# Attention into a gated MLP on one core: first keys and queries two tokens a partition, softmax sums by TensorE, value products with queries on partitions

## The chip, the cores and the metric

One core of a Trainium2 chip runs the whole kernel. The metric is device microseconds of one execution. Three runs of the kernel before took 704.2, 705.42 and 707.07 us, median 705.42. The profile is of one more execution, which took 703.89 us.

## The reference

Attention over 4 batches, 8 heads, 768 tokens, heads of 64, all f32. A query sees the keys less than 16 tokens away, and, beside those, one summary of every block of 32 keys (their maximum by component) whose value is the block's mean. Both share one softmax. The output, as 3072 tokens of 512, goes through a product of two linear maps and a third.

```python
k_sum = k.reshape(B, H, nb, block, D).max(axis=3)
v_sum = v.reshape(B, H, nb, block, D).mean(axis=3)
scores_l = scale * np.matmul(q, k.transpose(0, 1, 3, 2))
mask_l = np.abs(pos[:, None] - pos[None, :]) < window
scores_s = scale * np.einsum('bhsd,bhnd->bhsn', q, k_sum)
scores_s = scores_s + np.log(block)
...
a = a / (np.sum(a, axis=-1, keepdims=True) + 1e-09)
...
a = x @ w_a
b = x @ w_b
return (a * b @ w_out).astype(np.float32)
```

x is 3072 x 512, w_a and w_b are 512 x 1536, w_out is 1536 x 512.

## The kernel before, in words

The tokens are cut into 12 units of 256 (u, three to a batch), a unit into two chunks of 128 (g or t). The hidden width is cut into 12 parts of 128 (f). A pair (u, f) is an item: 24 products of 128x128 by 256 columns (the ups, L959), a multiplication on DVE, a split in a high and a low part on ACT and DVE, and 6 products of 512 columns (the downs, L995). Items of units 0 and 1 alternate while the weights come in; then each unit runs its 12 items. Numbers keep near f32 precision by a split in two fp32r parts: the weights are split on the chip (`convert`, from L271), 18 tiles j of two parts each: a scaled copy on ACT (L294), four steps on DVE (L309 or L315, L320, L327, L333), a rounding to the first part on ACT (L369), and two steps on POOL (L374, L380). `raw` is a weight tile as it comes from memory, `w` its two parts.

Attention of a chunk: the keys lie transposed in `kT`, 160 columns for each 128 tokens, with copies of the summaries in them (L436). For units 0 and 1 (`first_attention`, from L769) nothing is there yet, and the chain is this. Six loads bring 128 tokens of keys each, a token to a partition; TensorE turns each by four transposes (`turn`, L401) into a PSUM bank; ACT copies it into `kT` in two pieces (L460, L462) and DVE takes the blocks' maxima (L470). The queries are turned in the same way and scaled on ACT (L833). TensorE puts the mask into two banks by a product with the identity (L598) and adds the scores (L610, 16 products of 64x64 tiles, four beside each other). DVE takes the maximum of each row (L643), ACT the exponentials with their sums (L655, eight for each chunk, each followed by a read of its accumulator), DVE adds 1e-9 (L664), inverts (L670) and makes diagonal matrices of the result (L677). TensorE turns and scales the weights in one product with these (L698), ACT copies them (L710), TensorE multiplies by the values (L739; the result has channels on partitions, which the items need), and ACT and DVE split it (L747, L750) into `x`. The block means of the values come from twelve products with a matrix of 1/32 (L852).

Banks: o0 to o3 and c0, c1 (with buffer numbers 71 to 74, 77, 78), h0, h1 (75, 76). During this chain o0 and o1 serve chunks 0 and 2, o2 and o3 chunks 1 and 3, c0 and c1 the conversion of weights.

The order is written out ahead of time by the class `Work` (L22): every operation is recorded with an engine, a rank, an estimated duration and the names that it reads and writes, and `emit` lists them, always for the engine that is free first the ready operation of lowest rank. Each engine then runs its list strictly in order, and so do the loads, which all are issued on SP. The ranks around the change are those of L230 and those given to the loads:

```python
CHAIN, FIRST, CONVERT, NEXT, SOON, PREP, LATER = 0, 1, 2, 2.3, 5, 5.5, 6
...
rank = CONVERT + j / 4
...
for i, rank in enumerate((8, 9, 17, 17.5, 19, 20)):
    load_part(i, rank)
```

FIRST is the rank of unit 0's attention, NEXT unit 1's. A turn (product on TensorE) has rank FIRST too, values and scores rank -1.

Of the kernel before, what the change touches and what calls it, by code (L numbers as in the profile page):

```python
# [9 lines left out]
F32 = mybir.dt.float32  # L10
# [74 lines left out]
def attention_moe(  # L85
# [10 lines left out]
    nc = tc.nc  # L96
# [16 lines left out]
    SIGNS = 2  # L113
    AHEAD = (7, 9, 17)
# [75 lines left out]
    qTs = sb([P, NP, P], "qT")  # L190
    nml = [sb([P, 2, 2, NP], f"nml{i}") for i in range(2)]
# [38 lines left out]
    CHAIN, FIRST, CONVERT, NEXT, SOON, PREP, LATER = 0, 1, 2, 2.3, 5, 5.5, 6  # L230
# [40 lines left out]
    def convert(j):  # L271
# [81 lines left out]
        for hs in spans:  # L353
# [13 lines left out]
            act(  # L367
                rank - 0.5, 0.25 + 0.37 * len(hs), f + rk, hi,
                lambda ms=ms, f8=f8: nc.scalar.copy(out=parted(0)[:, ms], in_=f8),  # L369
            )  # L370
# [73 lines left out]
    def first_keys():  # L444
        n = P // BLK
        for i in range(S // P):
            x, key = spot(i // 2)
            x, key = x[:, i % 2 * 512 : (i % 2 + 1) * 512], key[i % 2]
            load(
                i, 262.0, 215, (), [key], x.rearrange("p (h d) -> p h d", d=D),  # L450
                heads(k[0, :, i * P : (i + 1) * P, :]),
            )
            bk = ("c0", "c1", "o2", "o3")[i % 4]
            pe(FIRST, 0.85, [key], [bk], lambda bk=bk, x=x: turn(bank[bk], x))
            c0 = PER * i

            def put(lo, bk=bk, c0=c0):
                tr = bank[bk].rearrange("p (c x) -> p c x", x=P)
                if lo:
                    nc.scalar.copy(out=kT[:, :, c0 + 16 : c0 + WIN], in_=tr[:, :, : WIN - 16])  # L460
                else:
                    nc.scalar.copy(  # L462
                        out=kT[:, :, c0 + P : c0 + PER + 16], in_=tr[:, :, WIN - 16 :]
                    )

            act(FIRST, 0.43, [bk], [f"kTl{i}"], lambda put=put: put(True))
            act(FIRST, 0.33, [bk], [f"kTh{i}"], lambda put=put: put(False))
            dve(
                FIRST, 0.6, [bk], [f"ksi{i}"],
                lambda bk=bk, i=i: nc.vector.tensor_reduce(  # L470
                    out=ks[:, :, i * n : (i + 1) * n],
                    in_=bank[bk].rearrange("p (c n x) -> p c n x", n=n, x=BLK),
                    axis=AX.X, op=ALU.max,
                ),
            )
# [598 lines left out]
```

## Time and profile before

| | |
|---|---|
| median of three runs | 705.42 us |
| the profiled execution | 703.89 us |
| its span, first to last instruction | 702.2 us |
| PE busy | 682.5 us, 97% |
| DVE busy | 439.8 us, 63% |
| ACT busy | 271.2 us, 39% |
| POOL busy | 182.3 us, 26% |
| mean granted clock of TensorE | 0.995 |
| read from memory, written | 47.12 MB, 6.29 MB |

PE is TensorE's products, PEld its weight loads, which overlap them; DVE is VectorE, ACT ScalarE, POOL GpSimd, SP the engine that issues loads. A row of a group or of the timeline names the line, the engine, the operation, and out<-in by the program's names, then the shape; x and a number counts records, and an f32 product makes two records where a transpose makes one. The ends of products are modelled, and the last of a row includes the way through the array, so that a row is some 0.2 us longer than the time to the next one. "Idle" and an arrow name what the engine waited for.

### The profile page before, as it was taken

Reading aid. Unit: us, or ns where it says so; the run is one execution under the profiler, and the core shown is the slowest. Engines: PE = TensorE matmul, PEld = TensorE weight load, DVE = VectorE, ACT = ScalarE, POOL = GpSimd, SP = SyncE. Lnnn points to the kernel's source line nnn. Section 1 sums busy time; section 2 is a strip of 40 time slices with the busy share of each in tenths; the row PEclk is TensorE's granted clock in tenths of the full one; section 3 lists DMA queues with packets and bytes.
Section 4 is the critical chain, followed back from the end, with each engine's and each line's share of the span. In section 5 each row is a group of like instructions: output and inputs, shape, how many; then the busy total and the mean of one; then the engine's idle time right before and its main releaser. Section 6 shows DMA issues by size and latency. Waiting matters only on the chain.

```text
span 702.2 us, 15117 instructions
## 1 busy us (share of the span) xinstructions
PE 682.5 (97%) x6000; PEld 626.5 (89%) x6000; DVE 439.8 (63%) x992; ACT 271.2 (39%) x815; POOL 182.3 (26%) x220
## 2 busy tenths in 40 slices
PE   6889999999999999999999999999999999999997
PEld 3768998898999999999999999999999999999996
DVE  2899899897767777767665776762762662311221
ACT  2998787532424332333332323332331431211211
POOL 5269878652442440113110101110110110000000
PEclk9989999999999999999999999999999999999999
DMA  9989835165224245132210330310310100000000
GB/s 227 280 182 291 301 80 155 27 141 125 64 74 98 70 99 116 32 58 78 54 24 17 69 67 2 87 24 1 84 24 1 54 21 1 31 1 1 31 1 31
DMA packets 154943, 54.84 MB, mean 78 GB/s; under 512 B 132456, under 2 KB 147816, under 8 KB 154872
## 3 DMA queue, kind: packets, MB, share of 16 engines
q1 hardware_dynamic: 154872, 53.88, 32.0%
q8 instruction: 47, 0.77, 0.5%
q14 instruction: 24, 0.20, 0.1%
HBM read 47.12 MB, written 6.29 MB: 76 GB/s over the span
## 4 chain that ended last, share of the span: by engine, by line
PE 85%; DVE 7%; ACT 4%; DMA 2%; issue 1%; POOL 0%; SPq 0%; POOLq 0%; DVEq 0%; ACTq 0%
PE h L959 51%; PE o L995 27%; PE c L739 2%; PE c L610 2%; PE o L739 2%; DVE pt L725 1%; DMA raw<-in_moe_w_b_dram 1%; PE o L610 1%; ACT s L655 1%; DVE c L327 1%; ACT c L294 1%; ACT S L294 1%; DVE ksum L470 1%; PE o L598 1%; DVE gl L984 0%
## 5 line engine op out<-in xcount | busy, mean ns | idle before, releaser
L959 PEld LDWEIGHTS h<-x,w 128*128 128x128 f32 x3456 | 413.9, 188 | 10.8 <-DVE c L327 0.2
L959 PE MATMUL h<-x,w 128*128 128x256 f32 x3456 | 416.3, 277 | 0.0
L979 DVE TENSOR_TENSOR h<-h,g 128x256 f32<-128x256 f32 x144 | 62.0, 430 | 163.7 <-ACT g L976 162.4
L976 ACT COPY g<-h 128x256 f32<-128x256 f32 x144 | 53.7, 373 | 277.6 <-PE h L959 276.8
L995 PE MATMUL o<-w,gh 128*128 128x512 f32 x576 | 158.0, 396 | 1.9 <-ACT gh L981 1.9
L995 PEld LDWEIGHTS o<-w,gh 128*128 128x128 f32 x576 | 98.8, 188 | 19.5 <-ACT gh L981 2.7
L725 DVE STREAM_TRANSPOSE pt<-s 32x256 f32<-32x256 f32 x240 | 104.7, 436 | 8.3 <-POOL s L685 4.0
L685 POOL TENSOR_TENSOR s<-s,nml 128x512 f32<-128x512 f32 x40 | 41.7, 1042 | 243.1 <-DVE nml L670 241.5
L995 PE MATMUL o<-w,gl 128*128 128x512 f32 x288 | 89.7, 393 | 0.0
L655 ACT ACTIVATE s<-s,nml 128x128 f32<-128x128 f32 x160 | 62.5, 393 | 49.5 <-DVE nml L643 46.8
L984 DVE TENSOR_TENSOR gl<-h,gh 128x256 fp32r<-128x256 f32 x144 | 60.5, 420 | 29.7 <-ACT gh L981 28.2
L981 ACT CAST gh<-h 128x256 fp32r<-128x256 f32 x144 | 53.5, 372 | 62.9 <-DVE h L979 62.6
L995 PEld LDWEIGHTS o<-w,gl 128*128 128x128 f32 x288 | 53.9, 188 | 11.7
L540 POOL TENSOR_TENSOR S<-S 96x512 f32<-96x512 f32 (+3 forms) x48 | 33.5, 698 | 49.6 <-DMA S<-in_v_dram 39.8
L655 ACT ACTIVATION_READ_ACCUMULATOR s<-s,nml 128x1 f32 x160 | 30.3, 190 | 0.0
L664 DVE TENSOR_SCALAR nml<-nml 128x4 f32<-128x4 f32 x40 | 11.5, 287 | 30.0 <-ACT s L655 30.0
L374 POOL TENSOR_TENSOR space<-space,w 128x1024 f32<-128x1024 f32 (+1 forms) x13 | 26.8, 2058 | 11.8 <-ACT w L369 10.9
L380 POOL TENSOR_TENSOR w<-space 128x1024 fp32r<-128x1024 f32 (+1 forms) x13 | 26.8, 2064 | 1.0
L294 ACT ACTIVATE S<-raw 128x1024 f16<-128x1024 f32 (+1 forms) x20 | 23.1, 1153 | 6.5 <-DVE S L309 4.6
L643 DVE TENSOR_REDUCE nml<-s 128x4 f32<-128x512 f32 x40 | 25.2, 667 | 0.0
L294 ACT ACTIVATE c<-raw 128x512 f32<-128x512 f32 x36 | 23.2, 645 | 4.0 <-DVE space L320 1.5
L436 POOL COPY kT<-ksum 128x144 f32<-128x144 f32 x16 | 4.7, 307 | 61.0 <-DVE ksum L518 55.0
(104 smaller groups left out, 478.0 us busy)
## 6 DMA issues: line engine op xcount, KB each, us to landing
raw<-in_moe_w_a_dram SPq DMA_DIRECT2D x12, 512.0 KB
raw<-in_moe_w_b_dram SPq DMA_DIRECT2D x12, 512.0 KB
raw<-in_moe_w_out_dram SPq DMA_DIRECT2D x12, 512.0 KB
out_dram<-S SPq DMA_DIRECT2D x24, 256.0 KB
qin<-in_q_dram SPq DMA_DIRECT2D x160, 32.0 KB
S<-in_v_dram SPq DMA_DIRECT2D x24, 192.0 KB
vw<-in_v_dram SPq DMA_DIRECT2D x18, 192.0 KB
kin<-in_k_dram SPq DMA_DIRECT2D x24, 100.0 KB
```

The lines of the kernel that those rows point to most:

```text
L294: nc.scalar.mul(out=zhalf[:, lo:hi] if out is None else out, in_=high.bitcast(F32), mul=2.0**-112)
L540: lambda: nc.gpsimd.tensor_tensor(out=out, in0=i0, in1=i1, op=ALU.add),
L655: lambda h=h, c=c, sums=sums: nc.scalar.activation(s[h][:, c, :], x[h][:, c, :], AF.Exp, bias=m[:, 0, h, c : c + 1], scale=1.0, accum_out= ...
L685: lambda h=h, r=r: nc.gpsimd.tensor_tensor(out=s[h], in0=s[h], in1=r[:, :, None].broadcast_to([P, NP, P]), op=ALU.mult,),
L725: lambda js=js, qs=qs: nc.vector.transpose(out=pv[js, :, qs], in_=sv[qs, :, js]),
L739: nc.tensor.matmul(ps[h * D : (h + 1) * D, c, es], vw[e][:, 2 * c + h, :], d[:, h, c, es], start=True, stop=True, tile_position=(0, h * D),)
L959: nc.tensor.matmul(ps, w[:, c, part, :], x[xpart][:, c, :], start=(i == 0), stop=(i == n - 1))
L976: act(CHAIN, 0.38, [hk], [gk], lambda: nc.scalar.copy(out=g, in_=pa))
L979: lambda: nc.vector.tensor_tensor(out=pa, in0=pb, in1=g, op=ALU.mult),
L981: act(CHAIN, 0.41, [hk], [ghk], lambda: nc.scalar.copy(out=gh, in_=pa))
L984: lambda: nc.vector.tensor_tensor(out=gl, in0=pa, in1=gh.bitcast(F32), op=ALU.subtract),
L995: nc.tensor.matmul(bank[ok[j]], (gh if first else gl)[:, js], w[:, :, part, :], start=(f == 0 and first and part == 0), stop=(f == NF - 1 ...
```

## The change

- Keys of batch 0 come in three loads of 256 tokens, and the queries of unit 0 in one, with two consecutive tokens a partition, so that a row in memory is 512 bytes, not 256. TensorE turns the even and the odd tokens apart (a half each), by eight products of 64 columns, two beside each other in the array (`turn_paired`, now L465). ACT puts each half into `kT` at every second column by three copies, DVE takes each half's block maxima, and one more operation joins them.
- In the first two units, ACT's exponentials no longer sum. The weights are turned unscaled by transposes; TensorE sums them by products with a column of ones, 1e-9 added by a first product (`total`), and multiplies them with the values so that queries, not channels, lie on partitions (`weigh`). DVE inverts the sums and scales the result, and TensorE turns it back for the split.
- POOL adds the two tokens of a partition of the values first, so the block means need six products, not twelve.
- POOL and not ACT rounds the first parts of weight tiles 0 and 1.
- The masks wait until the first keys are turned; unit 1's rank goes from 2.3 to 1.5, and the first weight tile's loads from ranks 8 and 9 to 5 and 5.5 (the queries have 6). Later units are as before; their code is only written more shortly.

```diff
+    FIRSTS = 2
...
+    ones = sb([P, 1], "ones")
+    nc.vector.memset(ones, 1.0)
+    small = sb([P, H], "small")
+    nc.vector.memset(small, 1e-9)
...
-    CHAIN, FIRST, CONVERT, NEXT, SOON, PREP, LATER = 0, 1, 2, 2.3, 5, 5.5, 6
+    CHAIN, FIRST, CONVERT, NEXT, SOON, PREP, LATER = 0, 1, 2, 1.5, 5, 5.5, 6
...
+            if j < FIRSTS:
+                pool(
+                    rank - 0.5, 0.1 + 0.55 * len(hs), f + rk, hi,
+                    lambda ms=ms, f8=f8: nc.gpsimd.tensor_copy(out=parted(0)[:, ms], in_=f8),
+                )
...
-            bk = ("c0", "c1", "o2", "o3")[i % 4]
-            pe(FIRST, 0.85, [key], [bk], lambda bk=bk, x=x: turn(bank[bk], x))
...
+    def load_paired(rank, key, x, src, row):
+        load(
+            rank, 524.0, 300, (), key, x.rearrange("p (h x) -> p h x", x=2 * D),
+            src[0, :, row : row + 2 * P, :].rearrange("h (p t) d -> p h (t d)", t=2),
+        )
+    def turn_paired(dst, x, y):
+        for c in range(NP):
+            for h in range(2):
+                nc.tensor.matmul(
+                    dst[h * D : (h + 1) * D, c * P : (c + 1) * P], paired(x)[:, 2 * c + h, y, :],
+                    ident, start=True, stop=True, tile_position=(0, h * D),
+                )
+    def first_keys(ksy, mk):
+        n = 2 * P // BLK
+        for m in range(S // P // 2):
+            x, key = spot(m)
+            load_paired(m, key, x, k, 2 * P * m)
+            for y in range(2):
+                bk = ("c0", "c1", "o2", "o3")[(2 * m + y) % 4]
+                pe(
+                    FIRST, 0.85, key, [bk] + ["first"] * (m == 0),
+                    lambda bk=bk, x=x, y=y: turn_paired(bank[bk], x, y),
+                )
...
+                def put(m=m, y=y, bk=bk):
+                    tr = bank[bk].rearrange("p (c i x) -> p c i x", c=NP, x=P // 2)
                     nc.scalar.copy(
+                        out=kper[:, :, 2 * m : 2 * m + 2, 16 + y : WIN : 2], in_=tr[:, :, :, :40]
                     )
+                    for i in range(2):
+                        c0 = PER * (2 * m + i) + P + y
+                        nc.scalar.copy(out=kT[:, :, c0 : c0 + 48 : 2], in_=tr[:, :, i, 40:])
+                act(FIRST, 0.9, [bk], [f"kT{m}{y}"], put)
+                dve(
+                    FIRST, 0.6, [bk, f"kT{m}{y}"], [f"ks{m}{y}"],
+                    lambda bk=bk, m=m, y=y: nc.vector.tensor_reduce(
+                        out=ksy[:, y, :, m * n : (m + 1) * n],
+                        in_=bank[bk].rearrange("p (c n x) -> p c n x", n=n, x=BLK // 2),
+                        axis=AX.X, op=ALU.max,
+                    ),
+                )
...
+        every = [f"{m}{y}" for m in range(3) for y in range(2)]
+        dve(
+            FIRST, 0.2, [f"ks{x}" for x in every] + [mk], [f"ks{c}" for c in range(NP)],
+            lambda: nc.vector.tensor_tensor(
+                out=ks, in0=ksy[:, 0], in1=ksy[:, 1], op=ALU.max
+            ),
+        )
         for c in range(NP):
...
-                d, dk = diag
-                dve(
-                    rank, 0.6, lk + [xk[h]], dk[h],
-                    lambda h=h, r=r, d=d: nc.vector.tensor_tensor(
-                        out=d[:, h], in0=ident[:, None, :].broadcast_to([P, NP, P]),
-                        in1=r[:, :, None].broadcast_to([P, NP, P]), op=ALU.mult,
-                    ),
-                )
...
-            def turned(h):
-                for c in range(NP):
-                    nc.tensor.matmul(
-                        bank[banks[h]][:, c * P : (c + 1) * P], s[h][:, c, :], d[:, h, c, :],
-                        start=True, stop=True,
-                    )
...
+        for h in range(2):
+            pe(
+                rank + 0.1, 0.9, ["first"], [banks[h]],
+                lambda h=h: nc.tensor.matmul(
+                    x[h], ident, mask[:, kind, None, :].broadcast_to([P, NP, P]),
+                    start=True, stop=False,
+                ),
+            )
+        pe(-1, 1.2, [*qk] + KT, banks, lambda: dots(t, qT, banks, False))
...
+                act(
+                    rank, 0.2, [f"{mk}m{h}", banks[h]], [sk[h]],
+                    lambda h=h, c=c: nc.scalar.activation(
+                        s[h][:, c, :], x[h][:, c, :], AF.Exp, bias=m[:, 0, h, c : c + 1]
+                    ),
+                )
...
+        def turned(h):
+            for c in range(NP):
+                nc.tensor.transpose(bank[banks[h]][:, c * P : (c + 1) * P], s[h][:, c, :], ident)
+        for h in range(2):
+            pe(-1, 0.6, [sk[h]], [banks[h]], lambda h=h: turned(h))
+            act(
+                rank, 0.6, [banks[h]], dk[h],
+                lambda h=h: nc.scalar.copy(
+                    out=d[:, h], in_=bank[banks[h]].rearrange("p (c x) -> p c x", x=P)
+                ),
+            )
+        ps = bank[banks[0]].rearrange("p (g d) -> p g d", d=D)
+        sums = bank[banks[1]][:, :H]
+        l = m[:, 1].rearrange("p h c -> p (h c)")
+        xn = s[0].rearrange("p c x -> p (c x)")
+        def total():
+            nc.tensor.matmul(sums, ident, small, start=True, stop=False)
+            for c in range(NP):
+                for h in range(2):
+                    g = 2 * c + h
+                    nc.tensor.matmul(
+                        sums[:, g : g + 1], d[:, h, c, :], ones, start=False, stop=g == H - 1
+                    )
+        def weigh():
+            for c in range(NP):
+                for h in range(2):
+                    g = 2 * c + h
+                    for e in range(2):
+                        es = slice(e * QT, (e + 1) * QT)
+                        nc.tensor.matmul(
+                            ps[es, g, :], d[:, h, c, es], vw[e][:, g, :],
+                            start=True, stop=True, tile_position=(0, e * QT),
+                        )
+        pe(-1, 0.5, dk[0] + dk[1], [banks[1]], total)
+        pe(-1, 1.1, dk[0] + dk[1] + vk, [banks[0]], weigh)
+        dve(
+            rank, 0.15, [banks[1]], [f"{mk}l"],
+            lambda: nc.vector.reciprocal(out=l, in_=sums),
+        )
+        dve(
+            rank, 0.6, [banks[0], f"{mk}l"], [sk[0]],
+            lambda: nc.vector.tensor_tensor(
+                out=xn.rearrange("p (g d) -> p g d", d=D), in0=ps,
+                in1=l[:, :, None].broadcast_to([P, H, D]), op=ALU.mult,
+            ),
+        )
+        pe(-1, 0.6, [sk[0]], [banks[1]], lambda: turn(bank[banks[1]], xn))
+        split(u, t, banks[1])
...
+        ksy = x[:, 512 + P + 16 : 512 + P + 16 + 2 * NP * NS]
+        first_keys(ksy.rearrange("p (t c n) -> p t c n", t=2, c=NP), mk)
+        q0, qk = spot(3)
+        load_paired(6, qk, q0, q, 0)
...
+        for y in range(2):
+            pe(FIRST, 0.85, qk, [f"h{y}"], lambda y=y: turn_paired(bank[f"h{y}"], q0, y))
+            act(
+                FIRST, 0.6, [f"h{y}"], [yk[y]],
+                lambda y=y: nc.scalar.mul(
+                    out=both[:, :, y :: 2],
+                    in_=bank[f"h{y}"].rearrange("p (c x) -> p c x", x=P), mul=0.125,
+                ),
+            )
...
-            for y in range(2):
-                nc.tensor.matmul(
-                    bank["h0"][:, g * 256 : (g + 1) * 256], mean[:, 16 - 8 * i : 16 - 8 * i + P],
-                    vin[n][0][:, :, y * D : (y + 1) * D],
-                    start=(i == y == 0), stop=(i == 2 and y == 1),
-                )
+            nc.tensor.matmul(
+                bank["h0"][:, g * 256 : (g + 1) * 256], mean[:, 16 - 8 * i : 16 - 8 * i + P],
+                vin[n][0][:, :, :D], start=(i == 0), stop=(i == 2),
+            )
 
         for n in range(6):
-            pe(FIRST + 0.5, 1.0, [vin[n][1], mk], ["h0"], lambda n=n: means(n))
+            x, key = vin[n]
+            pool(
+                FIRST, 0.7, [], [key],
+                lambda x=x: nc.gpsimd.tensor_tensor(
+                    out=x[:, :, :D], in0=x[:, :, :D], in1=x[:, :, D:], op=ALU.add
+                ),
+            )
+            pe(FIRST + 0.5, 0.5, [key, mk], ["h0"], lambda n=n: means(n))
...
-    for i, rank in enumerate((8, 9, 17, 17.5, 19, 20)):
+    for i, rank in enumerate((5, 5.5, 17, 17.5, 19, 20)):
```

More of the change, by code (lines that the diff above doesn't have):

```diff
@@ L442, in attention_moe, with paired @@
     KT = [f"kT{c}{x}" for c in range(NP) for x in "ks"]
[L444 to L451, printed above, removed]
-            )
-            bk = ("c0", "c1", "o2", "o3")[i % 4]
-            pe(FIRST, 0.85, [key], [bk], lambda bk=bk, x=x: turn(bank[bk], x))
[L455 to L461, printed above, removed]
+    def paired(x):
+        return x.rearrange("p (h t d) -> p h t d", t=2, d=D)
```

286 lines of the change are left out of this document (122 added, 164 removed).

## The prediction

> **What bounds the kernel now.** I read the stage table first, then TensorE's timeline, then the waits, then the groups by line. The stage table of before (from to: length, busy us of each engine with counts, granted clock, DMA share, GB/s):
>
> ```profile
> 0.00:18.30 18.30, 10.62 (x42) 6.21 (x42) 5.12 (x8) 5.92 (x15) 9.90 (x58) 1.00 1.10 229
> 18.30:62.50 44.20, 38.67 (x420) 31.89 (x421) 41.61 (x79) 40.45 (x110) 25.33 (x17) 0.92 1.00 246
> 62.50:150.00 87.50, 85.63 (x692) 79.19 (x691) 80.74 (x155) 61.26 (x129) 70.92 (x43) 1.00 0.54 151
> 150.00:702.20 552.20, 547.54 (x4851) 509.18 (x4849) 312.37 (x751) 163.52 (x564) 76.11 (x105) 1.00 0.21 48
> ```
>
> The columns are PE, PEld, DVE, ACT, POOL. After 62.5 us PE is busy 99% of the time; from 18.3 to 62.5 DVE is (41.61 of 44.2, 94%), ACT close behind it. TensorE's timeline and its waits from 62 us on give the point where that changes:
>
> ```profile
> 62.54 5.62 PE L959 MATMUL h<-x,w 128*128 128x256 f32 x48
> PE o L995 <- ACT gh L981: 1.9, 2, 1.2
> ```
>
> 62.54 us is the start of item (0,2), the third product item. From there PE runs almost through: it waits 1.9 us at two down-products and little else. The change touches nothing that PE does behind this point, and in both programs PE has issued the same two items ahead of it. So the change is worth what it moves the start of (0,2), plus any new wait behind it. Everything below works out that one time.
>
> One more thing lies in that stretch. The stage table around PE's longest pause there:
>
> ```profile
> 43.60:47.00 3.40, 1.18 (x11) 1.02 (x10) 3.17 (x9) 3.27 (x15) 0.14 (x1) 1.00 0.82 272
> 47.00:53.90 6.90, 6.18 (x52) 5.57 (x51) 6.59 (x12) 6.87 (x15) 5.36 (x3) 0.51 1.18 281
> ```
>
> PE was busy for only 1.18 of 3.4 us, and then had half its clock for 6.9 us.
>
> **The first stage: loads, keys, queries.** Rates (last column) of the first 5 us, and by what SP's issues then brought: 256-byte rows at 2 to 8 us, weights at 12 to 14, 512-byte rows of values at 16 to 18:
>
> ```profile
> 0.00:5.00 5.00, 0.55 (x1) 0.50 (x2) 0.97 (x2) 1.28 (x1) 3.80 (x27) 1.00 0.68 134
> 2.00:8.00 6.00, 3.55 (x4) 1.40 (x5) 0.01 (x1) 0.09 (x1) 4.79 (x29) 1.00 1.24 219
> 12.00:14.00 2.00, 1.08 (x5) 0.71 (x6) 0.90 (x2) 1.01 (x4) 0.00 (x0) 1.00 1.09 339
> 16.00:18.00 2.00, 0.89 (x9) 0.65 (x6) 0.69 (x1) 1.24 (x4) 0.64 (x3) 1.00 1.22 290
> ```
>
> 134 GB/s over 5 us is 0.67 MB, at 219 GB/s 3.1 us: bytes flow from 1.9 us. Two tokens a partition make 512-byte rows. The first of three key loads (0.52 MB at 290) has landed at about 4.0, the last at 7.4. Two weight loads (ranks 5 and 5.5) now pass the queries on SP: 1.05 MB at 339 is 3.1 us, then 1.8 for the queries, 12.4 us. Before: 2.1 MB at 219 from 1.9, 11.5 us. The queries lose 0.9 us, covered by the key turns and masks ahead of them on PE (to 16.4, below); without that cover it would cost the 0.9.
>
> TensorE's prices, from the timeline (start, length, group):
>
> ```profile
> 4.45 3.78 PE L598 MATMUL o<-mask,ident 128*128 128x512 f32 x4 [4.45 <-POOL mask L173]
> 10.68 0.66 PE L401 MATMUL c<-ident,space 128*128 128x128 f32 x4
> 18.29 1.10 PE L610 MATMUL o<-kT,qT 64*64 64x128 f32 x32 [1.40 <-POOL kT L436]
> 19.25 1.10 PE L610 MATMUL o<-kT,space 64*64 64x128 f32 x32
> 23.94 1.13 PE L698 MATMUL o<-pt,s 128*128 128x128 f32 x8
> 28.30 1.03 PE L852 MATMUL h<-space,space 128*128 128x256 f32 x4
> 30.80 1.01 PEld L739 LDWEIGHTS h<-pt,vw 128*64 128x64 f32 x32
> 30.80 1.15 PE L739 MATMUL h<-pt,vw 128*64 128x64 f32 x32
> 34.34 1.98 PE L598 MATMUL o<-mask,ident 128*128 128x512 f32 x4 [0.71 <-ACT qT L833]
> ```
>
> Two masks took 3.78 us at the start and 1.98 later: PE starts at half speed. A turn of 128 tokens (four transposes) is about 0.55 us. The change turns with eight plain products of 64 columns by 128 instead, two records each. One 128-column record is about 0.12 us (L698, eight in 1.13 with the tail). L739 shows 32 records on two column halves in 1.15, 0.03 each for 64 columns, so two run beside each other: 16 records of 0.06 make 0.95 us a half. One after another they would take 1.9; below 0.95 nothing in the trace points.
>
> PE now begins with the first keys at 4.0, not with masks. I let it warm at 9.5, as far behind its first work as the rows allow (the masks were slow from 4.45 to 8.2): 2.9 halves at 1.9 us, then 3.1 at 0.95, end 12.4. ACT's three copies a half and DVE's maximum keep that pace; before, they took turns on one bank:
>
> ```profile
> 10.31 0.32 ACT L462 COPY kT<-c 128x192 f32<-128x192 f32 x1 [0.76 <-DVE ksum L470]
> 10.52 0.43 ACT L460 COPY kT<-c 128x320 f32<-128x320 f32 x1
> 17.36 1.05 POOL L436 COPY kT<-ksum 128x144 f32<-128x144 f32 x4 [5.92 <-DVE ksum L470]
> ```
>
> 0.43 and twice 0.2 is 0.85 us on ACT. The keys' part ends some 3 us earlier, but PE isn't ready to use it: the four masks stand behind the key turns now (4 x 1.0), then two query halves (1.9) and two mean products (1.0): the scores start at 19.3 us, against 18.29. So the early keys gain nothing; the one thing gained is that DVE converts weights meanwhile:
>
> ```order
> L470 TENSOR_REDUCE ksum<-c_78 128x4x4
> L315 TENSOR_SCALAR space_195<-c_77 128x512
> L320 SCALAR_TENSOR_TENSOR space_195<-c_77,space_195 128x512
> L643 TENSOR_REDUCE nml_184<-o_71 128x4
> L643 TENSOR_REDUCE nml_184<-o_72 128x4
> ```
>
> These are DVE's rows up to the first score maxima (L643), before. Now, with L728 the maxima and raw_211 the first weight tile:
>
> ```order
> L499 TENSOR_REDUCE space_196<-c_78 128x4x8
> L508 TENSOR_TENSOR ksum<-space_196 128x96
> L320 TENSOR_SCALAR space_199<-c_77 128x512
> L325 SCALAR_TENSOR_TENSOR space_199<-c_77,space_199 128x512
> L332 TENSOR_SCALAR c_78<-space_199 128x512
> L320 TENSOR_SCALAR space_199<-c_77 128x512
> L338 SCALAR_TENSOR_TENSOR space_199<-raw_211,c_78 128x512
> L325 SCALAR_TENSOR_TENSOR space_199<-c_77,space_199 128x512
> L332 TENSOR_SCALAR c_78<-space_199 128x512
> L338 SCALAR_TENSOR_TENSOR space_199<-raw_211,c_78 128x512
> L728 TENSOR_REDUCE nml_188<-o_71 128x4
> L728 TENSOR_REDUCE nml_188<-o_72 128x4
> ```
>
> Eight conversion steps stand ahead of the maxima, not two.
>
> **The second stage: sums by PE, queries on partitions.** What leaves DVE and ACT, and what POOL pays for such work: groups by line and shape up to 62.5 us (busy, mean ns of one, idle before), and four timeline rows:
>
> ```profile
> L677 DVE TENSOR_TENSOR pt<-ident,o 128x512 f32<-128x512 f32 x4 | 2.7, 687 | 0.2
> L677 DVE TENSOR_TENSOR space<-ident,o 128x512 f32<-128x512 f32 x4 | 2.7, 686 | 0.1
> L670 DVE RECIPROCAL o<-o 128x4 f32<-128x4 f32 x8 | 1.5, 190 | 0.2
> L664 DVE TENSOR_SCALAR o<-o 128x4 f32<-128x4 f32 x8 | 1.3, 165 | 0.2
> L327 DVE TENSOR_SCALAR c<-space 128x512 int32<-128x512 int32 x10 | 6.9, 689 | 0.1
> 20.04 2.47 DVE L643 TENSOR_REDUCE nml<-o 128x4 f32<-128x512 f32 x4
> 20.76 0.37 ACT L655 ACTIVATE s<-o,nml 128x128 f32<-128x128 f32 x1
> 21.02 0.17 ACT L655 ACTIVATION_READ_ACCUMULATOR s<-o,nml 128x1 f32 x1
> 21.22 0.37 ACT L655 ACTIVATE s<-o,nml 128x128 f32<-128x128 f32 x1
> L369 ACT CAST w<-space 128x512 fp32r<-128x512 f32 x4 | 2.4, 613 | 0.0
> L710 ACT COPY pt<-o 128x512 f32<-128x512 f32 x4 | 2.5, 621 | 0.0
> L870 POOL COPY space<-vw 32x512 f32<-32x512 f32 x2 | 1.2, 609 | 11.7 <-ACT vw L864 11.7
> L374 POOL TENSOR_TENSOR space<-space,w 128x512 f32<-128x512 f32 x4 | 5.1, 1284 | 1.9 <-ACT w L369 1.9
> ```
>
> DVE loses 2.7 + 2.7 + 1.5 + 1.3 = 8.2 us and gets four reciprocals (0.19) and four 128x512 products (0.69), 3.5. With the eight early steps (8 x 0.69 = 5.5) its 41.6 us of the stretch become about 31.4. ACT: an exponential and its accumulator take 0.46 us from start to start; alone 0.15 to 0.26 (the accumulator starts 0.26 behind it), I take 0.2, the nearer to the 192-element copy's 0.21. 32 x 0.26 = 8.3 less, and 2.4 of roundings go to POOL: 40.4 becomes under 30. POOL gets four copies (0.61) and six sums of half of L374's size (0.64), 6.3 us on 25.3 of 44.2: hidden, since its first weight parts are due only at item (0,0).
>
> PE gets the difference. For chunk 0, from the means (L852, now L930) to the value products (L739, now L778), before and now; o_71 to o_74 are its PSUM banks:
>
> ```order
> L698 MATMUL o_71<-pt,s 128x128 x4
> L698 MATMUL o_72<-pt,s 128x128 x4
> L852 MATMUL h_75<-space_191,space_192 128x256 x2
> L698 MATMUL o_73<-space_188,space_191 128x128 x4
> L852 MATMUL h_75<-space_191,space_192 128x256 x2
> L401 MATMUL o_71<-ident,space_188 128x128 x4
> L698 MATMUL o_74<-space_188,space_191 128x128 x4
> L739 MATMUL h_76<-pt,vw_165 64x64 x2
> ```
>
> ```order
> L748 MATMUL o_71<-ident,s 128x128 x4
> L748 MATMUL o_72<-ident,s 128x128 x4
> L930 MATMUL h_75<-space_195,space_196 128x256
> L764 MATMUL o_72<-small,ident 128x8
> L768 MATMUL o_72<-ones,pt 128x1 x8
> L778 MATMUL o_71<-vw_165,pt 64x64
> ```
>
> The plain products with a diagonal become transposes (1.0 us a bank to 0.55). New are the sums (L764, L768: nine products, 18 weight loads for hardly a column) and, behind the value products, a turn back of 0.55 (L412). The sums' price: a load and record of 128 columns is at most 0.12 (L698, there bound by the columns), at least twice the 0.03 of a 64-column load (L739): 1.1 to 2.2 us a chunk. I take the middle, 1.65. The Trainium skill (TensorE: Matmul & The Clock Gate, LDWEIGHTS) gives a load its columns divided by 1.2, 107 ns for 128: by that the sums would be 1.9, an estimate from that page. No run here shows such loads without columns behind them.
>
> Ups and downs are from the chain of waits, undisturbed:
>
> ```profile
> 72.50 1.37 PE o L995 x6
> 73.88 2.75 PE h L959 x24
> ```
>
> PE's list from the first scores to (0,2): scores 4 x 0.95, means 4 x 0.5 (half as many products, six fewer, 3 us), turns 8 x 0.55, sums 4 x 1.65, values 4 x 1.05, turns back and of the later queries 6 x 0.55, masks 4 x 1.0, ups 2 x 2.75, downs 2 x 1.37: 3.8 + 2.0 + 4.4 + 6.6 + 4.2 + 3.3 + 4.0 + 5.5 + 2.7 = 36.5 us. That is more than DVE's 31 or ACT's 30: the bound passes to PE, and 19.3 + 36.5 = 55.8 is the floor.
>
> Above the floor stand PE's waits, since the order is fixed. Chunk 0: its scores end at 20.3, two maxima (2.47 / 4 each) and the last exponentials at 22.9, when PE has done chunk 1's scores and three means (22.7): 0.2. Its sums need two copies of ACT with a conversion copy between them, 0.5 each from start to start: 0.9. Its turn back waits 1.0 for DVE, which reads the sums (L787) and then does three conversion steps of 0.69 ahead of the product. Chunk 2's turns: 0.3, for an item's copy among its exponentials. The last stands here, DVE between chunks 2 and 3, before and now:
>
> ```order
> L677 TENSOR_TENSOR pt<-ident,o_71 128x512
> L643 TENSOR_REDUCE nml_185<-o_73 128x4
> L643 TENSOR_REDUCE nml_185<-o_74 128x4
> L979 TENSOR_TENSOR h_75<-h_75,g_173 128x256
> L327 TENSOR_SCALAR c_78<-space_193 128x512
> ```
>
> ```order
> L728 TENSOR_REDUCE nml_189<-o_73 128x4
> L787 RECIPROCAL nml_188<-o_72 128x8
> L728 TENSOR_REDUCE nml_189<-o_74 128x4
> L338 SCALAR_TENSOR_TENSOR S_190<-raw_310,c_78 128x512
> L314 SCALAR_TENSOR_TENSOR space_199<-c_77,S_191 128x512
> ```
>
> Chunk 3's second maximum now queues behind chunk 2's reciprocal, which waits for PE's sums. Behind the sums' end come that reciprocal (0.25), the maximum (0.65), two conversion steps (1.4) that free the bank for a copy of ACT (0.5), and three exponentials behind it (0.75): 3.55 us, in which PE has only the value products (1.05): a wait of 2.5. Sum 4.9 us; (0,2) starts at 60.7, 1.8 earlier than 62.54. The profiled execution took 703.89 us, so 702.1; the median of the three runs shown is 705.42, 1.5 above it, so 703.6.
>
> **Rivals.** *The waits close* (chance 0.34). Sums at 1.1 us take 2.2 off PE's list, and 0.55 each off the waits of chunk 0 and chunk 3; a clock that warms 1.7 us sooner gives 0.9. (0,2) at 56.5, 6.0 off: 699.4. For it speaks that DVE and ACT then have 10 us to spare; against it the fixed order.
>
> *PE's clock falls again* (0.23). The wait of 2.5 us ahead of chunk 3's turns is as long as the pause in the table above (2.2 idle of 3.4) that half clock followed. Then turns, an up and sums run twice as long over 6.9 us: 3.4 us more than forecast, 707.0; with the sums at 2.2 another 3.3, 710.3, slower. The Trainium skill (TensorE: Matmul & The Clock Gate, What's actually happening) has the clock halve after an idle window of about 3.4 us and come back after a busy one; the trace agrees on two such lengths at half clock (6.9 us), but fell with PE busy a third of its window.
>
> *The paired turns don't pair* (0.10), the case on the other side. If the two column halves run one after another, a half is 1.9 us warm. The six key halves end at 18.1 instead of 12.4, the query halves cost 1.9 more: +7.6, so 711.2. It decides from 1.2 us a warm half on (0.95 + 1.8/8); above 1.6 the kernel is measurably slower. L739's 0.03 speaks against it; L468 being no transposes, for it.
>
> **How the numbers follow.** Forecast 0.33, the others 0.34, 0.23, 0.10. About 0.5%, 3.5 us, is what a measurement of this kernel can tell from no change. Faster: 0.34. Same: 0.33 and 0.16 of the clock's. Slower: 0.07 of it and 0.10, 0.17. The range 698.5 to 709 leaves out about 0.1 on either side: the fastest end of the first rival, and the unpaired turns; both signs are in it, and the forecast's own range, with the sums' two ends, is 700 to 707.
>
> **What would show it.** Right: L468 at 0.95 a half when warm, first scores near 19.3, L768 near 1.65 a chunk, L787 waiting for it, PE's pause ahead of chunk 3's L748, (0,2) near 60.7, DVE no longer the busiest from 18 to 62. Wrong: scores before 17 or after 21, no pause there, or new waits of PE behind 62 us on weights (DVE or ACT late).

## The result, and the profile after

The changed kernel took 726.25 us (median of 4 runs, 723.34 to 729.63), the kernel before 705.94 on the same chip (4 runs, 704.20 to 707.07). The ratio is 1.029, interval 1.024 to 1.034: slower by 20 us, far outside the forecast of 698.5 to 709. The profiled execution took 726.35 us, its span is 724.6.

First where the time went. The start of item (0,2) in the timeline after, and the stage table from there to the end, after and then before:

```profile
67.01 5.92 PE L1034 MATMUL h<-x,w 128*128 128x256 f32 x48
```

```profile
67.01:724.60 657.59, 653.07 (x5541) 605.83 (x5539) 390.55 (x904) 225.33 (x693) 146.62 (x147) 1.00 0.24 60
```

```profile
62.54:702.20 639.66, 633.13 (x5541) 588.36 (x5539) 393.11 (x905) 224.75 (x692) 147.00 (x147) 1.00 0.26 62
```

(0,2) starts at 67.01 instead of 62.54, 4.5 us later. Behind it PE handles exactly as many records of products as before (5541), at a granted clock of 1.00 in both, waits less (4.5 us against 6.5), and yet needs 17.9 us more. So four fifths of the loss lie where the prediction had said that nothing could change. The chain of waits shows that it is no stall. The 24 ups of an item, then six downs and the next 24 ups, after (the rows of before have 2.75 and 1.37):

```profile
78.88 2.88 PE h L1034 x24
81.76 1.40 PE o L1070 x6
83.15 2.88 PE h L1034 x24
```

0.13 us more an item, times the 142 items behind (0,2), is 18.5 us: every up is a little slower, all the time. The downs add a little, and the shorter waits take as much off again.

Now the stretch ahead of (0,2), by the stage table of after, with the four windows around the clock's two falls:

```profile
18.30:62.50 44.20, 40.25 (x427) 34.66 (x422) 31.36 (x53) 32.42 (x70) 25.49 (x23) 0.85 0.83 226
...
24.55:27.96 3.41, 2.20 (x19) 1.80 (x17) 1.38 (x2) 3.36 (x7) 2.63 (x4) 1.00 0.94 288
27.96:34.79 6.83, 6.83 (x57) 6.70 (x57) 5.32 (x9) 3.59 (x10) 2.53 (x4) 0.50 0.77 215
...
48.45:51.86 3.41, 3.41 (x68) 3.22 (x58) 2.16 (x6) 2.77 (x4) 2.55 (x2) 1.00 1.14 314
51.86:58.68 6.82, 4.65 (x29) 4.47 (x26) 6.52 (x12) 6.71 (x15) 5.23 (x3) 0.50 0.94 269
```

Before, the clock was halved once in this stretch (6.9 us from 47.0), now twice, 6.83 us each. Ahead of the second fall PE was busy for all of the window (3.41 of 3.41), so a wait in that window can't be its cause. The same two windows for the sums' line alone (length, PE and PEld with counts, granted clock, DMA share, GB/s):

```profile
24.55:27.96 3.41, 1.41 (x13) 1.44 (x13) 1.00 0.94 288
48.45:51.86 3.41, 1.93 (x16) 1.87 (x16) 1.00 1.14 314
```

Most of what PE did ahead of both falls were products with one moving column. The steps of the prediction, in the timeline of after:

```profile
11.39 1.93 PE L468 MATMUL c<-ident,space 128*64 128x128 f32 x32
19.84 0.43 PE L686 MATMUL o<-kT,space 64*64 64x128 f32 x5
...
21.70 2.25 ACT L736 ACTIVATE s<-o,nml 128x128 f32<-128x128 f32 x8 [2.16 <-DVE nml L728]
...
49.08 1.93 PE L768 MATMUL o<-ones,pt 128*128 128x1 f32 x16
...
54.34 1.97 PE L748 MATMUL o<-ident,space 128*128 128x128 f32 x8 [2.17 <-ACT space L736]
```

Two key halves take 1.93 us warm with the tail, 0.97 each, the scores start at 19.84, and the wait ahead of chunk 3's turns is 2.17: these were foreseen at 0.95, 19.3 and 2.5.

### The profile page after: what moved, and what is told of

Its sections match the earlier page's. It is cut to its first block, busy times and chain, and to the rows that moved or that the text cites. A ratio compares the mean times of both kernels' runs of the same rounds, so it can differ in the third digit from the quotient of the medians.

```text
span 724.6 us, 15385 instructions
## 1 busy us (share of the span) xinstructions
PE 711.1 (98%) x6140; PEld 655.3 (90%) x6140; DVE 434.2 (60%) x979; ACT 266.4 (37%) x785; POOL 188.7 (26%) x230
## 4 chain that ended last, share of the span: by engine, by line
PE 90%; DVE 4%; ACT 2%; DMA 2%; issue 1%; SPq 0%; DVEq 0%; ACTq 0%
PE h L1034 52%; PE o L1070 26%; PE c L819 2%; PE o L686 2%; PE c L686 2%; PE o L819 1%; PE o L768 1%; PE o L719 1%; PE c L468 1%; DVE c L332 1%; DVE pt L704 1%; DMA raw<-in_moe_w_b_dram 1%; PE o L748 1%; DMA raw<-in_moe_w_out_dram 1%; ACT s L736 1%
## 5 line engine op out<-in xcount | busy, mean ns | idle before, releaser
L1034 PEld LDWEIGHTS h<-x,w 128*128 128x128 f32 x3456 | 430.8, 189 | 10.9 <-issue 0.3
L1034 PE MATMUL h<-x,w 128*128 128x256 f32 x3456 | 434.4, 283 | 0.0
L1070 PE MATMUL o<-w,gh 128*128 128x512 f32 x576 | 159.7, 399 | 0.7 <-ACT gh L1056 0.6
L666 DVE TENSOR_SCALAR nml<-nml 128x4 f32<-128x4 f32 x40 | 9.4, 234 | 30.0 <-ACT s L658 30.0
```

Source lines behind the costliest of these rows:

```text
L1034: nc.tensor.matmul(ps, w[:, c, part, :], x[xpart][:, c, :], start=(i == 0), stop=(i == n - 1))
L1070: nc.tensor.matmul(bank[ok[j]], (gh if first else gl)[:, js], w[:, :, part, :], start=(f == 0 and first and part == 0), stop=(f == NF - 1 ...
```

## Experiments on the ups: where the weights lie

Theory A: the two new tiles, `ones` (4 bytes a partition) and `small` (32 bytes), lie between `x` and the weight tiles, and in units of 32 bytes they push all weights 64 bytes away from `x`; the ups read both at once. Theory B: something in the changed instruction list slows them. In bytes of a partition, `x` and the first buffer of the weights begin at 31360 and 63936 before and at 31360 and 64000 after, so they lie 32576 and 32640 apart. So the kernel before got an unused tile and nothing else, and the changed kernel one more:

```diff
+    sb([P, 16], "pad")      # before_pad64, after_pad64; [P, 32] in before_pad128
```

In before_padx64 the same 64 bytes stand ahead of `x`, so that `x` and the weights move together.

> The kernel before, unchanged but for the same unused tile of 64 bytes ahead of nml: the weight tiles move to 0 modulo 128, where the changed kernel has them. Theory A: ups at 119 to 120 ns, 144 items x 24 x 5.2 ns = 18 us more, 721 to 726 us. Theory B: 705 us, ups at 114 ns.

> The kernel before with an unused tile of 128 bytes: all behind it moves, but the weights stay at 64 modulo 128. Theory A: no change, 704 to 707 us, ups at 114 ns. If any shift of the weights by itself, or the place modulo 256, slows the ups (theory A2): 721 to 726 us.

> The changed kernel with one unused tile of 64 bytes a partition behind the new tiles ones and small, so that the weight tiles begin at 64 modulo 128 again, as before the change, while x stays at 0. Theory A (the place of the weight tiles against x slows every up, 114 to 119.5 ns): ups back at 114 ns, the 17.9 us behind item (0,2) gone, 0.3 to 0.8% over the kernel before: 707 to 711 us. Theory B (something in the order or the other engines' work of the changed program slows the ups): ups stay at 119 to 120 ns, 724 to 729 us.

> The kernel before with the unused 64 bytes ahead of x: x, g, gh, gl and the weights all move, the weights to 0 modulo 128 and x to 64, so that they stand to each other as before. If the place of the weights against x decides (A, relative): 704 to 707 us, ups at 114 ns. If the place of the weights alone decides (A, absolute): 721 to 726 us, ups at 119 to 120 ns.

Measured against 705.66 us for the kernel before (13 runs): before_pad64 722.05, ratio 1.024 (1.021 to 1.027); before_pad128 718.78, 1.020 (1.015 to 1.024); after_pad64 724.63, 1.027 (1.023 to 1.031); before_padx64 704.71, 0.999 (0.997 to 1.000). The ups of one item by the chain of waits, of before_pad64, before_pad128 and before_padx64:

```profile
317.09 2.88 PE h L960 x24
```

```profile
302.57 2.82 PE h L960 x24
```

```profile
312.46 2.75 PE h L960 x24
```

An unused tile of 64 bytes makes the old kernel as slow in the ups as the changed one, and moving both operands together costs nothing. So the distance counts, and not the list. Two expectations failed: I had taken the effect to repeat with 128 bytes, and it doesn't. By itself after_pad64 lies in the range of Theory B (724 to 729 us); but its weights lie 128 bytes farther from `x` than before, and its ups take 117.8 ns from start to start, as those of before_pad128 do. Then the tiles of the changed kernel were put ahead of `x`:

```diff
+    ones = sb([P, 1], "ones")
+    nc.vector.memset(ones, 1.0)
+    small = sb([P, H], "small")
+    nc.vector.memset(small, 1e-9)
     xs = [[sb([P, NP, CH], f"x{i}_{p}", F32R) for p in range(2)] for i in range(2)]
```

> The changed kernel, its two new tiles (the column of ones and the 1e-9 tile) allocated ahead of x instead of behind it, so that weights and x lie as far apart as in the kernel before (32,576 bytes of a partition). Nothing else is changed. Theory A (the distance of weights and x sets the rate of the ups): ups 114.3 ns from start to start, item period 4.120 us, and behind the start of (0,2) 638 to 640 us, as before; (0,2) itself still starts near 67.0, since the clock still falls twice ahead of it: 706 to 710 us, ratio 1.001 to 1.006. Rival B (something in the changed list behind (0,2) slows the ups): ups near 119.5 ns, 722 to 728 us.

It took 711.42 us (711.07 to 712.22), ratio 1.009 (1.007 to 1.011). The ups and the stage behind the start of (0,2), which in this run is at 68.66:

```profile
300.05 2.75 PE h L1034 x24
```

```profile
68.66:709.40 640.74, 634.16 (x5541) 588.95 (x5539) 393.15 (x904) 225.13 (x693) 146.48 (x147) 1.00 0.25 61
```

640.7 us instead of 657.6, and 2.75 again. Theory B is out: 14.8 us of the 20 came from the place of two tiles of 36 bytes. The total lies just above the range expected (706 to 710 us), and the profiled execution has three falls of the clock ahead of (0,2), not the two expected. Three more distances were tried, on a later version of the kernel (after_mv_wide, below), with an unused tile of 192, 256 and 32 bytes ahead of `nml`, behind `x`:

> As after_mv_wide, with an unused tile of 192 bytes a partition ahead of nml, so that weights and x lie 192 bytes farther apart than in the kernel before. What the distance does is known at 0 (114.3 ns from up to up), 64 (119.5) and 128 (117.8) more. If the rate repeats with 256 bytes and falls off on both sides of a best place, 192 gives about what 64 gave, 118 to 120 ns and 721 to 726 us; if it keeps coming down towards 256 or 512, 114 to 117 ns and 704 to 715 us; if the place before isn't the best one, under 113.5 ns and under 702 us.

> As after_mv_wide, with 256 bytes a partition more between weights and x. If the rate repeats with 256 bytes: 114.3 ns from up to up, 703 to 707 us. If it repeats with 512 bytes (all tiles of weights and x begin a multiple of 512 bytes apart), another rate than at 0: 117 to 121 ns and 714 to 728 us, or, if the place before isn't the best one, under 113.5 ns and under 702 us.

> As after_mv_wide, with 32 bytes a partition more between weights and x. The rate so far: 114.3 ns at 0 and 256 bytes more, 119.5 at 64, 117.8 at 128, 119.7 at 192. If lines of 64 bytes or less count, 32 lies between 0 and 64: 115 to 119 ns, 707 to 722 us. If the place before is not the best, under 113.5 ns and under 702 us. If only whole steps of 64 count, 114.3 ns and 703 to 707 us.

One run each: 723.23, 705.38 and 719.76 us. The first two are what a period of 256 bytes gives, and the third shows that 32 bytes already count. Their ups of an item, in the same order:

```profile
303.56 2.87 PE h L1034 x24
```

```profile
312.99 2.75 PE h L1034 x24
```

```profile
302.94 2.82 PE h L1034 x24
```

All together (mean time from the start of one up, or of one down, to the next within an item, worked out from the records behind 300 us):

```
bytes more than before    0      32     64     128    192    256
ns from up to up          114.3  118.1  119.5  117.8  119.7  114.3
ns from down to down      232.1  236.3  235.5  236.7  235.1  232.2
```

The rate of the ups is the same at 0 and at 256 and 3 to 5% worse at the four distances between. The downs lose 1 to 2% at the same four, where the weights have moved by the same bytes against their other operand (`gh` and `gl`, allocated behind `x`). All pieces of weights and `x` that an up reads begin a multiple of 512 bytes from the start of their tile, and the tiles a multiple of 4096 bytes from the first of their kind, so that one distance holds, but for multiples of 512, for all 3456 ups. The Trainium skill (TensorE: Matmul & The Clock Gate, Step-by-step: what each phase is for) has two independent read ports, so that loading the next weights takes nothing from the product that runs. These runs disagree: with nothing but the distance changed, an up costs up to 5.4 ns more. Which of the two reads is held up, and what in the memory makes 256 bytes special, wasn't tried.

## Experiments on the clock

Theory C: a window of 3.41 us filled mostly with one-column products counts as idle. Rival D: PE's waits alone make the clock fall. All kernels here start from after_mv. after_mv_wide widens the sums' products (the loads and their number stay):

```diff
-    ones = sb([P, 1], "ones")
+    ones = sb([P, D], "ones")
...
-            nc.tensor.matmul(sums, ident, small, start=True, stop=False)
...
-                        sums[:, g : g + 1], d[:, h, c, :], ones, start=False, stop=g == H - 1
+                        wide[:, 2 * c + h, :], d[:, h, c, :], ones, start=True, stop=True
```

> As after_mv, but each product of the sums moves 64 columns of ones instead of one (the 1e-9 that a first product adds is left out; the sums stand in every 64th column). As many weight loads and as many products. Theory C (a window full of one-column products counts as idle for the clock): neither of the two falls of the clock at 28 and 52 us, or at most one, (0,2) starts at 60.5 to 63.8, the sums take about as long in the warm clock, 699 to 705 us. Rival D (the clock falls because PE waits for ACT and DVE in these stretches, whatever the products' width): two falls as in after_mv, (0,2) at 67 or later, 706 to 712 us.

It took 704.61 us (10 runs, 702.40 to 706.18), 6.8 less than after_mv; against the kernel before 0.998 (0.996 to 1.000). Its profile, which is of the fastest of the ten executions, has no fall:

```profile
18.30:60.64 42.34, 37.77 (x455) 31.37 (x453) 33.60 (x58) 32.87 (x70) 29.19 (x23) 1.00 1.01 246
...
24.95 2.00 PE L767 MATMUL o<-ones,pt 128*128 128x64 f32 x16 [1.21 <-ACT pt L754]
60.64 5.62 PE L1033 MATMUL h<-x,w 128*128 128x256 f32 x48
```

64 columns take about as long as one (2.00 us a chunk, 1.93 with one), and (0,2) starts at 60.64. But seven of the ten executions have a mean granted clock of 0.995 to 0.998, so a short fall stays in most of them. The profile of wide_pad256, which differs only by its unused tile, has one from 48.83 to 52.24. The next kernel took the sums off PE again: ACT sums beside its exponentials (`accum_out`), DVE adds 1e-9 and inverts.

> As after_mv, but the sums are taken by ACT beside its exponentials again, as before, and DVE adds 1e-9 and inverts: the sums' products on PE are gone. Theory C: no fall that follows a window of sums; PE loses about 2.3 us a chunk and ACT gains 8 reads of about 0.19 us a chunk, so (0,2) at 59 to 63.5 with no fall or one: 698 to 705 us. Rival D: with the sums gone PE waits more for ACT, and the clock falls at least once as in the kernel before (there at 47.05): (0,2) at 62.5 to 67, 702 to 709 us.

712.97 us (712.76 to 713.19), no gain, and above the ranges of both theories. With no sums on PE at all, the clock fell behind a window in which PE was busy for 0.89 us, since its turns waited 3.6 us for ACT:

```profile
22.23:25.65 3.42, 0.89 (x7) 0.55 (x5) 1.90 (x4) 3.14 (x9) 3.14 (x5) 1.00 0.94 215
25.65:32.47 6.82, 5.49 (x47) 4.68 (x48) 5.22 (x9) 4.82 (x21) 4.35 (x5) 0.50 1.06 331
```

So waits do it too, and here they are waits for ACT's exponentials, which read their accumulators again. Then the masks were not held back any more, with one-column sums (after_mv_masks) and with wide ones (wide_masks):

```diff
-                rank + 0.1, 0.9, ["first"], [banks[h]],
+                rank + 0.1, 0.9, [], [banks[h]],
```

> As after_mv, but the mask products of the first chunks don't wait for the first keys any more, so PE has work earlier: it should turn warm at about 9.5 instead of 10.9 us. Theory C: the sums' windows still count as idle, so two falls, (0,2) within 1 us of after_mv's (about 67), time within 1.5 us of after_mv's. Rival E (the falls hang on how the clock's windows happen to lie over PE's waits, and a shift of the start moves them): one fall or none, (0,2) 63.8 or earlier, 3 to 6 us faster than after_mv.

> after_mv_wide with the first chunks' mask products not held back behind the first keys either. Theory C (with 64 columns a product the clock doesn't fall, and what was left to lose is the ordinary path of the first stage): no fall of the clock, ups 114.3 ns, and the start of (0,2), 60.6 in after_mv_wide, moves by no more than 1 us either way, since the first chunk's scores hang on the keys: 702.5 to 705.5 us, ratio 0.995 to 0.999. Rival E (earlier work of PE brings the whole stage forward): (0,2) at 57 to 59.5, 700 to 702 us.

705.93 us (ratio 1.002, 1.000 to 1.004) and 705.83 (1.000, 0.999 to 1.001). Early masks alone win 5.5 us on after_mv; with them, wide sums win nothing more. Theory C had expected the first within 1.5 us of after_mv and the second without a fall, and both expectations failed. The first still has two falls, but of 3.41 us each, and the second has one, which the stage table shows:

```profile
41.83:45.25 3.42, 1.84 (x39) 1.28 (x36) 3.42 (x7) 2.04 (x5) 1.30 (x1) 1.00 0.89 236
45.25:48.66 3.41, 2.13 (x18) 2.05 (x18) 0.79 (x3) 3.05 (x6) 3.33 (x2) 1.00 1.21 285
48.66:52.07 3.41, 3.37 (x39) 3.15 (x38) 3.13 (x6) 2.94 (x8) 0.08 (x1) 0.50 1.23 258
```

The length of the wait doesn't decide by itself either: the clock passed a window with PE busy for 1.84 us (scores and turns) and fell behind the next, with 2.13 us (sums of 64 columns). So the width was tried where PE has no waits. probe_cols puts five bursts of 36 extra products between dense items of after_mv_wide, probe_share 17 shorter ones of one column:

```diff
         def hidden():
+            cols = {50: 64, 66: 32, 82: 16, 98: 4, 114: 1}.get(n, 0)
+            for _ in range(36 if cols else 0):
+                nc.tensor.matmul(pa[:, :cols], ident, ones[:, :cols], start=True, stop=True)
```

> after_mv_wide with five bursts of 36 extra products, each with its own weight load, ahead of the ups of five items far behind the start, where PE doesn't wait and the clock is 1.00: 64 columns wide at item 50, 32 at 66, 16 at 82, 4 at 98, 1 at 114 (their results are overwritten). A burst lasts about 9 us (0.25 us a product, as in the sums), two windows of 3.41 and more. Theory C (few moved columns count as idle): half clock within or right behind the burst at item 114 and the narrower of the others, none at 64 columns; about 45 us for the bursts and 3 us for each fall, 750 to 765 us. Rival D (only waits count): no fall at any burst, 749 to 752 us.

> after_mv_wide with 17 bursts of 6, 8, 10 or 12 extra one-column products (about 1.5, 2.0, 2.5 and 3.0 us) ahead of the ups of every sixth item from 42 on, dense work on both sides. Theory C: falls behind some of the bursts of 8 and more (8 is one chunk's sums), more of the long ones than of the short, each 3.4 us or twice that at half clock; none without a burst. 740 to 765 us. Rival D: none at all, 742 to 746 us.

One run each, 769.89 us (both theories had expected less, 765 at most) and 752.84. probe_cols: the bursts of 64 columns and of one in the timeline, and the stage table over the first and over the half clock at the other four:

```profile
283.06 8.15 PE L1048 MATMUL h<-ones,ident 128*128 128x64 f32 x72
...
622.86 11.76 PE L1048 MATMUL h<-ones,ident 128*128 128x1 f32 x72
```

```profile
283.06:291.21 8.15, 8.15 (x74) 8.14 (x73) 2.33 (x10) 0.13 (x1) 0.62 (x2) 1.00 0.53 80
...
367.37:381.03 13.66, 13.66 (x66) 13.66 (x66) 0.00 (x0) 0.00 (x0) 0.00 (x0) 0.50 0.00 0
456.12:466.36 10.24, 10.24 (x49) 10.24 (x49) 0.00 (x0) 0.00 (x0) 0.00 (x0) 0.50 0.00 0
541.45:551.69 10.24, 10.24 (x50) 10.24 (x50) 0.00 (x0) 0.00 (x0) 0.00 (x0) 0.50 0.09 15
626.79:640.44 13.65, 13.65 (x64) 13.55 (x64) 0.00 (x0) 0.37 (x1) 0.00 (x0) 0.50 0.00 1
```

That settles the core of Theory C: products of few columns make the clock fall without any wait. PE and its weight loads are busy all but without a gap in every row; with 64 columns the clock stays at 1.00, with 32, 16, 4 and 1 it falls to half for 10 to 14 us. In probe_share none of the eight bursts of 6 or 8 products (two records each) was followed by a fall, three of the four of 10, and four of the five of 12. One of these, by its own line, and the window behind it:

```profile
364.67:367.41 2.74, 2.73 (x24) 2.65 (x23) 1.00 0.02 6
368.20:371.61 3.41, 0.00 (x0) 0.00 (x0) 0.50 0.00 0
```

So one chunk's sums (8 products, 1.9 us) don't make the clock fall by themselves between dense work. The windows can be counted in steps of 3.41 us from any change of the clock. By that count all seven falls behind these bursts follow a window with 2.18 to 2.62 us of one-column products, and no window with 2.04 us or less of them is followed by a fall. The two longer bursts without a fall lay across two windows, with 2.04 and 1.81 us in the fuller one.

In the kernel there is less of them. Ahead of the first fall of after stand 1.41 us of sums and 1.21 of waiting. Ahead of the second stand 1.93 us of sums and no wait, but value products that move 64 columns each. For the second, waits are out: after_mv has such a fall too (37.42 to 40.83, with PE busy for all of the window ahead of it and 1.93 us of sums in it), while in wide_masks the sums of 64 columns with the value products (55.49 to 58.90, PE busy for 2.95 us) leave the clock at 1.00. So both theories hold a part. How a window's other products (turns, values) are weighed wasn't tried, so no rule for a whole window comes out of these runs.

Last, wide_fill puts one product of 512 columns, whose result is overwritten, behind the wide sums of chunk 2, where PE waited for values:

```diff
+        def fill():
+            nc.tensor.matmul(
+                bank[banks[0]].rearrange("p (c x) -> p c x", x=P), ident,
+                mask[:, 0, None, :].broadcast_to([P, NP, P]), start=True, stop=True,
+            )
         pe(-1, 0.5, dk[0] + dk[1], [banks[1]], total)
+        if t == G:
+            pe(-1, 0.5, dk[0] + dk[1], [banks[0]], fill)
```

> after_mv_wide with one more product of 512 columns (mask by identity, about 1.0 us, overwritten by what follows) between the sums and the value products of chunk 2, where PE waited 1.0 to 1.5 us for values. Theory C and D alike (the one fall left near 48 us comes from that stretch's idle time): no fall, (0,2) at 60.3 to 61.2, 702 to 704 us, ratio 0.995 to 0.998. If that stretch isn't what makes the clock fall: a fall near 48 us in some executions as before, 704 to 706 us.

704.84 us (12 runs), ratio 0.998 (0.997 to 0.999): with after_mv_wide the best version, 0.2% under the kernel before and some 3% under the changed one. The fall near 48 us is gone from the profile, but this execution has one elsewhere, behind a window with wide sums and 1.2 us of waiting:

```profile
24.72:28.13 3.41, 2.21 (x19) 1.81 (x17) 1.38 (x2) 3.36 (x7) 2.62 (x4) 1.00 0.77 147
28.13:31.54 3.41, 3.41 (x41) 3.18 (x40) 2.72 (x6) 1.44 (x6) 1.58 (x2) 0.50 0.93 296
```

This is the window of the first fall of after, with PE busy as long (2.21 us and 2.20) and sums of 64 columns in place of one. So that fall can't be put down to the sums' width: it comes with wide ones too, though for 3.41 us and not 6.83.

## Why the prediction was wrong

**The step that failed** is "The change touches nothing that PE does behind this point", and with it that the change is worth what it moves the start of (0,2). PE's list behind that point is indeed the same, 5541 records. But the change moved the operands: two tiles for 36 bytes changed the distance of weights and `x` by 64 bytes, and each of 3456 ups took 5 ns more. 14.8 us by the medians (726.25 to 711.42), 16.9 by the spans behind (0,2). Nothing in the profile of before shows it. The two tiles stand in the diff, and the prediction gave their place no term and no rival. Why the distance has a price stays open.

**The clock.** The rest up to the forecast was a rival that came true (that PE's clock falls again), and by more than it was given: with the tiles put back the changed kernel takes 711.42 us, and this rival was 707.0 to 710.3. It supposed one fall, from the wait of 2.5 us; there were two in the profile of after and three in that of after_mv, and none of after's came from that wait, which lies behind the second. The sums took part in the second, ahead of which PE was busy throughout. The forecast itself priced no fall, though the kernel before has one in this stretch. The rule of the Trainium skill cited in the prediction has an idle window halve the clock; probe_cols shows that idle there doesn't mean that no product runs.

**The sum for (0,2)** comes out when both are taken away, but with luck: forecast 60.7, in the profile of after_mv_wide 60.64. That is the fastest of ten executions; the median is 704.61 us against 703.6 forecast, and in the profiles of wide_masks and wide_fill, each with one short fall, (0,2) starts at 62.49 and 62.77, about where it did before (62.54). Its terms were less exact than the sum, and their errors cancel. The sums were mis-sized: 1.65 us a chunk forecast, 1.85 to 2.0 measured, and 0.25 more for their first product (which after_mv_wide leaves out); the 1.9 that the prediction gives as an estimate from the Trainium skill (TensorE: Matmul & The Clock Gate, LDWEIGHTS) was nearer. An exponential alone is 0.27 from start to start (8 in 2.25 us less the tail), not 0.2. Against that the scores start at 18.48 in after_mv_wide instead of 19.3, so the list took 42.2 us from there instead of 41.4. The waits were right in size, 4.6 us there, 4.9 forecast, but not all in place: values of unit 1 (1.0 us, for their load) were not in it, and the wait ahead of chunk 3's turns is 0.9 there.

**What else was said.** The turns pair (0.97 us a half). DVE's work from 18.3 to 62.5 us is 31.36 us, forecast 31.4; ACT's 32.42, forecast under 30. No wait of PE in this stretch ends with POOL. By the waits of after, L787 waits for the sums in all four chunks:

```profile
DVE nml L787 <- PE o L768: 5.8, 4, 1.7
```

Without the new distance and with wide sums the change gains about a microsecond (705.48 to 704.61 in after_mv_wide, 705.93 to 704.84 in wide_fill), less than the 3.5 us that the prediction took to be measurable. No part of it was tried alone, so how this gain is made up stays open.

## What to carry to other kernels

A new tile is part of a change even if nothing slow reads it: compare the addresses of the operands of the hot products before and after, and allocate small new tiles where they shift nothing. Where a profile shows a group of unchanged instructions with the same count, the same clock and a longer mean, look at where its operands lie before looking for a wait. And products that move few columns keep PE busy in the records without keeping its clock up, so make them wider if that costs no time. Near a wait that may not be enough: the clock fell here with wide sums too.

## What the runs showed of the hardware

- The rate of 256-column products with a weight load each hangs on the distance of their two operands: 114.3 ns at 0 and 256 bytes more than before (32576), 117.8 to 119.7 at 32, 64, 128 and 192 more.
- A product of one column and one of 64 take about the same time with a load of 128 columns each (0.11 to 0.12 us a record), but in bursts of 36 between dense work only the wide one holds the clock: no fall at 64 columns, half clock for 13.7, 10.2, 10.2 and 13.7 us at 32, 16, 4 and 1.
- Between dense work, the clock fell behind the windows of 3.41 us in which one-column products took 2.18 us or more (seven), and behind none in which they took 2.04 or less (one run of 17 bursts).
